# Ordering PSUM evacuations, step pacing and put-off products in a fused attention and MLP kernel

## The chip, the core and the metric

The kernel runs on one core of one Trainium2 chip. The core has five engines that each work through a queue of their own in order: PE (TensorE, matrix products; PEld is its weight load, which overlaps the products), DVE (VectorE), ACT (ScalarE), POOL (GpSimd) and SP (SyncE, which here only issues DMAs). They are ordered among each other by semaphores alone. PE writes its products into PSUM, which has eight banks; here three of them serve as accumulators for the products this document is about. The metric is the device time of one execution in microseconds (us), the median over runs. Times of single instructions come from a profile of one execution.

## The reference

```python
xn = _layernorm(x)                                   # x: 2048 x 640
# A: sliding-window attention, H = 32 heads of Dh = 20, window W = 256
qkv = (xn @ wqkv).reshape(B, S, 3, H, Dh)
scores = jnp.einsum("bhqd,bhkd->bhqk", q, k) * (Dh ** -0.5)
mask = (i - j >= 0) & (i - j < W)
p = _softmax(jnp.where(mask, scores, -1e9))
s = jnp.einsum("bhqk,bhkd->bhqd", p, v) @ wo
# B: MLP with a squared ReLU, F = 1536
h = xn @ w1 + b1
h = where(h > 0, h, 0) ** 2
g = _silu(h @ w2 + b2)
out = x + s * g
```

All tensors are fp32. The kernel splits operands into a high and a low part (hi, lo) and forms three products (hi hi, hi lo, lo hi) for each one of the reference.

## The kernel before

**Stages.** The first 120 us normalise x, transpose it, and compute v for all heads and q, k for the first group of heads. Then a loop of 268 steps (`steps`, L1128) runs the attention of 16 pairs of heads (p), 16 blocks of queries (q) each. In its gaps it runs a filler (L873): the q and k of the other four groups of heads, and then the MLP in eight blocks, each with a first product (hps) and a second one (yps). What comes after the loop is the rest of the filler and the output projection (`out_filler`, wops).

**Row halves.** Within the loop every product has 64 contraction rows. Each is issued as two matmuls, one on rows 0 to 63 of the array (the front) and one on rows 64 to 127 (the back), which can run side by side. The fronts of a job run first. Its backs follow in a queue (`backlog`, for values `urgent`), beside the fronts of the jobs after it.

**The planner's clock.** The order on all engines is written while the program is built. `clock[0]` adds up the estimated cost of the fronts, `clock[1]` that of the backs, from the table COST (L44). `ahead` emits backs until `clock[1]` is LEAD ahead of `clock[0]`, and then one front. None of this exists on the chip: it only decides in which order instructions enter the queues.

**One step (L1149 to L1201).** First the scores of one block (sps), the transposed scores of the block nine steps back (stps), every fourth step the rows of maxima. Then DVE takes the maxima (junk, L503), ACT the exponentials (p, L549), and POOL masks p (L550, L552). Then comes an early piece of filler, then `low` (pl on DVE, L563), `flush()`, `tick()` (splitting of weights), `high` (ph on ACT, L557), then a late piece of filler, and in odd steps the products with v (`values`, ops). p has three buffers; pl is the last to read one. sps and stps have two banks each, both of which every step uses.

**Accumulator banks.** A filler job takes one of three banks (`Acc`, L659), 30 pairs of matmuls for hps (15 for q/k, 18 for yps), and then an evacuation reads the bank:

- q/k: shm on ACT (L112), slo on DVE (L113), two stores.
- hps, in two halves of 256 columns (`part`, L949): relu and hh on ACT, sq on DVE (L956), hl on POOL (L957). The second half is `rest`, in the list `late`.
- yps: one add on DVE (ysb, L990); a store after both halves of a row block.

When the last back of a job is emitted, `done` (L690) puts the evacuation into `pending` and notes the time in `ended`. `soon` (L635), called after each filler product, emits the late half when `clock[0]` is 2 x SOON past the last flush, and a pending evacuation when it is SOON (0.3) past its job's end. `flush` (also called once in the middle of every step) emits all that is waiting. `free` puts a bank back into the list when its evacuation has been emitted.

**Filler per step.** `fill(amount)` draws products until their nominal costs (0.213, 0.1065 and 0.133 a pair) reach the amount: 35% of `per` in the early piece, and 65% plus or minus SWING in the late one. A product whose operand is not evacuated yet (`product`, L1001) yields None, which ends the piece.

Of the kernel before, what the change touches and what calls it, by code (L numbers as in the profile page):

```python
# [16 lines left out]
P = 128  # L17
# [8 lines left out]
NB = 4  # L26
# [12 lines left out]
RAW = 3  # L39
EARLY_FILL = 0.35  # L40
SWING = 0.3
WARM = 22
# [7 lines left out]
LEAD = 0.15  # L50
SOON = 0.3

# [6 lines left out]
def attn_mlp_kernel(ctx: ExitStack, tc, x, wqkv, wo, w1, b1, w2, b2, out):  # L59
# [571 lines left out]

    ended = deque()
    halved = [0.0]

    def soon():  # L635
        now = clock[0]
        if late and now >= halved[0] + 2 * SOON:
            flush(flushed[0])
        if ended and now >= ended[0][1] + SOON:
            flush(ended.popleft()[0])  # L640

    def flush(upto=None):
        halved[0] = clock[0]
        for f in late[:]:
            f()
        late.clear()
        while pending and (upto is None or flushed[0] < upto):
            flushed[0] += 1
            pending.pop(0)()
# [6 lines left out]

    banks = [0, 1, 2]

    class Acc:  # L659

        def __init__(self, n, name):
            while not banks:
                if pending or late:
                    flush()
                else:
                    drain(backlog, 1)
            self.bank, self.n = banks.pop(0), n
            self.tile = pmm.tile([P, n], F32, tag=f"mm{self.bank}", name=name)

        def free(self):  # L670
            banks.append(self.bank)

# [16 lines left out]
    def open_job(evac, *then):  # L689
        def done():  # L690
            pending.append(evac)
            ended.append((mark(), clock[1]))
            for f in then:
                f()
        job = Job(done)
        backlog.append(job)
        return job
# [175 lines left out]
    def filler():  # L873
# [5 lines left out]
        for g, b in order_qk:  # L879
# [9 lines left out]
            for w in "qk":  # L889
                hi, lo = (t() for t in ws[g][w])  # L890
                ps = Acc(BT, "qkps")

                def evac(ps=ps, w=w, g=g, b=b):
# [3 lines left out]
                    split(hi, lo, ps.tile)  # L897
                    ps.free()
                    posts.extend(qk_stores(w, slice(g * P, (g + 1) * P), slice(b * BT, (b + 1) * BT), hi, lo))
# [19 lines left out]
        for n, (hf, b) in enumerate(blocks):  # L919
# [10 lines left out]
            wt1 = w1t[hf]()  # L930
            hs, whole, nxt = {}, set(), []

# [7 lines left out]
            for th in range(2):  # L940
                for fp in range(NFH // 2):
                    ps = Acc(BT, "hps")

                    def evac(ps=ps, th=th, fp=fp, fi=hf * NFH + 2 * fp, hs=hs, whole=whole):
                        hh = [stg.tile([P, BT], F32R, tag="stg", name="hh"),
# [14 lines left out]
                        def rest():  # L960
                            part(1)
                            whole.add((th, fp))
                            ps.free()
                        late.append(rest)
                    job = open_job(evac, *([used] if (th, fp) == (1, NFH // 2 - 1) else []))
                    mms = [(i, lin1(wt1, (wp * KC + c) * FHALF + (2 * fp + i) * P, P), xb[xp][:, c * BT + th * MT:c * BT + (th + 1) * MT]) for i in range(2) for c in range(KC) for wp, xp in ((0, 0), (0, 1), (1, 0))]
# [9 lines left out]
            for tt in range(4):  # L976
# [4 lines left out]
                def start(nh, hf=hf, t=t, place=place, idx=4 * (n - NB) + tt, end=n == NB - 1 and tt == 3, n=n, tt=tt):  # L981
# [3 lines left out]
                    def evac():  # L985
# [4 lines left out]
                        nc.vector.tensor_add(ysb[:, sl], ps.tile, (yins[t] if hf else b2t)[:, sl])  # L990
                        ps.free()
                        if nh:
# [20 lines left out]
                for nh in range(2):  # L1013
                    job = start(nh)
                    for fc in range(NFH):
# [43 lines left out]
    def out_filler(wo_part):  # L1059
# [27 lines left out]
        for u in range(2 * NB):  # L1087
# [10 lines left out]
            for t2 in range(2):  # L1098
# [3 lines left out]
                for nh in range(2):  # L1102
# [21 lines left out]
                    pending.append(evac)  # L1124

    fl = filler()
    total = 8 * (KC - 1) * 15 * 0.213 + 2 * NB * (6 * 15 * 0.213 + 8 * 18 * 0.133)
    steps = NP * NT + LAG + 3  # L1128

    def fill(amount):  # L1130
        state[1] += amount
        while state[0] < state[1]:
            c = next(fl, None)
            if c is None:
                state[1] = state[0]
                return
            state[0] += c
            if state[2] < 10 ** 6:
                soon()

    per = total / (steps - 1)
    with tc.manual_schedule(engines={E_.PE, E_.Activation, E_.DVE, E_.Pool, E_.SP}):
# [6 lines left out]
        for s in range(steps):  # L1149
# [88 lines left out]
```

## Time and profile before

| | us |
|---|---|
| median of 3 runs | 956.03 (954.85 to 958.91) |
| the profiled execution, its own time | 955.41 |
| its span in the profile | 953.7 |
| mean granted clock of PE | 0.991 of full speed |

| stage (us of the span) | what runs |
|---|---|
| 0 to 121 | normalise, transpose, v, first q and k |
| 121 to 288 | attention steps, with the other q and k as filler |
| 288 to 862 | attention steps, with the MLP as filler |
| 862 to 954 | output projection |

How to read the lines that follow: an engine's busy time is given with its share of the span and its count of instructions. A group reads "line engine operation out<-in (partitions x elements)", then its count, its busy time, the mean length of one in ns, the idle time of the engine just before it, and what ended that idle time. A row of a timeline begins with the start and the length in us; "[2.33 <-DVE sq L956]" says that the engine sat idle for 2.33 us until the DVE instruction of line 956 that wrote sq had ended. Rows of one form that follow each other closely are merged (x4). A row of waits gives the total in us, how often, and the longest. The names of the tiles are those of the program: p, ph, pl are the exponentials and their two halves, hps and yps the MLP's accumulators, sps and stps the scores, ops the products with v.

### The profile page before, as it was taken

What the parts mean: (1) busy time and instruction counts of PE and PEld (TensorE: products, weight loads), DVE (VectorE), ACT (ScalarE), POOL (GpSimd) and SP (SyncE); (2) the same over time, 40 slices, a digit from 0 to 9 for tenths busy, and PEclk for the clock granted to TensorE, in tenths of its full rate; (3) what the DMA queues carried; (4) which work ended last, traced back from release to release, by engine and by line L of the source; (5) the groups of instructions that cost most, each with busy time, mean ns of one, the idle gap of its engine ahead of it and who ended that gap; (6) DMA issues with size and microseconds to landing.
All of it is one profiled execution on the core that took longest, in us unless ns stands there. A gap on an engine that the chain in (4) does not pass through costs nothing.

```text
span 953.7 us, 35554 instructions
## 1 busy us (share of the span) xinstructions
PE 898.4 (94%) x14368; PEld 850.3 (89%) x14368; DVE 757.3 (79%) x2085; ACT 648.0 (68%) x1240; POOL 507.4 (53%) x800
## 2 busy tenths in 40 slices
PE   8999999999999989999999889889989989989998
PEld 8999989998888889889899879789889989888998
DVE  7774378998999988878888889978888878864564
ACT  4444347887778967867968867967877967873231
POOL 5010004665556866766867756856776856761000
PEclk9999999999999999999999999999999999999999
DMA  7997788787686262354355244465265274054773
GB/s 250 285 399 276 233 258 255 223 253 252 202 262 193 70 208 85 75 195 112 80 187 147 73 139 121 112 190 151 73 195 156 52 221 124 10 191 142 268 284 126
DMA packets 106108, 169.95 MB, mean 178 GB/s; under 512 B 42072, under 2 KB 59608, under 8 KB 103384
## 3 DMA queue, kind: packets, MB, share of 16 engines
q1 hardware_dynamic: 105944, 167.68, 56.1%
q8 instruction: 113, 1.85, 0.9%
q14 instruction: 51, 0.42, 0.2%
HBM read 96.15 MB, written 70.91 MB: 175 GB/s over the span
## 4 chain that ended last, share of the span: by engine, by line
PE 59%; DVE 20%; ACT 12%; issue 6%; POOL 3%; DMA 0%; DVEq 0%; ACTq 0%; POOLq 0%
PE yps L481 14%; PE ops L481 8%; PE wops L654 7%; PE vps L232 7%; PE qkps L481 6%; DVE junk L503 6%; DVE pl L563 5%; ACT p L549 5%; PE hps L481 5%; PE sps L493 4%; DVE sq L956 3%; PE qkps L209 3%; PE stps L542 3%; ACT relu L953 2%; ACT ph L557 2%
## 5 line engine op out<-in xcount | busy, mean ns | idle before, releaser
L549 ACT ACTIVATE p<-stps,ebias 128x384 f32<-128x384 f32 (+2 forms) x512 | 258.5, 557 | 140.7 <-PE stps L542 62.2
L481 PE MATMUL yps<-w,hh 64*128 64x320 f32 x1536 | 256.9, 320 | 35.1 <-DVE sq L956 24.1
L503 DVE CUSTOM_DVE_ANT_0 junk<-sps,mask 128x384 bf16<-128x384 f32 (+2 forms) x512 | 250.3, 525 | 46.9 <-PE sps L493 30.0
L550 POOL TENSOR_SCALAR_AFFINE_SELECT p<-p 128x256 f32<-128x256 f32 x256 | 151.0, 590 | 234.4 <-ACT p L549 160.6
L563 DVE TENSOR_TENSOR pl<-p,ph 128x768 f16<-128x768 f32 (+2 forms) x256 | 247.8, 968 | 3.5 <-ACT p L549 2.3
L481 PE MATMUL hps<-xb,w 64*128 64x256 f32 x2520 | 236.5, 285 | 2.5 <-DVE ysb L990 2.5
L481 PEld LDWEIGHTS yps<-w,hh 64*128 64x128 f32 x1536 | 197.8, 190 | 43.9 <-DVE sq L956 27.8
L481 PEld LDWEIGHTS hps<-xb,w 64*128 64x128 f32 x2520 | 221.1, 187 | 4.1 <-DVE ysb L990 4.1
L557 ACT ACTIVATE ph<-p 128x768 f16<-128x768 f32 (+2 forms) x256 | 205.7, 804 | 0.0
L481 PE MATMUL ops<-vp,ph 64*128 64x61 bf16 x2880 | 203.8, 190 | 0.1
L481 PE MATMUL ops<-vp,pl 64*128 64x61 bf16 x2880 | 201.7, 189 | 0.0
L481 PE MATMUL yps<-w,hl 64*128 64x320 f32 x768 | 193.4, 320 | 0.0
L481 PEld LDWEIGHTS <-pl 64*128 64x128 f16 x2880 | 177.1, 94 | 0.1
L481 PEld LDWEIGHTS <-ph 64*128 64x128 f16 x2880 | 174.4, 94 | 2.2 <-PE stps L542 0.6
L552 POOL TENSOR_SCALAR_AFFINE_SELECT p<-p 128x256 f32<-128x256 f32 x224 | 133.6, 596 | 0.0
L493 PE MATMUL sps<-ks,qs 60*128 60x384 f32 (+2 forms) x512 | 124.7, 366 | 8.4 <-DVE mrow L526 3.7
L481 PEld LDWEIGHTS yps<-w,hl 64*128 64x128 f32 x768 | 122.9, 189 | 0.0
L542 PE MATMUL stps<-qs,ks 62*128 62x384 f32 (+2 forms) x512 | 110.7, 344 | 0.3 <-DMA qs<-mrow 0.2
L481 PE MATMUL qkps<-xT,wgkh 64*128 64x512 f32 x320 | 103.8, 400 | 0.0
L957 POOL TENSOR_TENSOR hl<-sq,hh 128x256 fp32r<-128x256 f32 x96 | 88.2, 925 | 29.0 <-DVE sq L956 23.5
L481 PE MATMUL qkps<-xT,wgqh 64*128 64x512 f32 x320 | 103.2, 399 | 0.0
L493 PEld LDWEIGHTS sps<-ks,qs 60*128 60x128 f32 x512 | 69.0, 187 | 24.3 <-DVE mt L503 15.3
(110 smaller groups left out, 1627.0 us busy)
## 6 DMA issues: line engine op xcount, KB each, us to landing
ks<-k_d SPq DMA_DIRECT2D x64, 240.0 KB
qs<-q_d SPq DMA_DIRECT2D x64, 240.0 KB
xb<-xs SPq DMA_DIRECT2D x12, 1280.0 KB
xs<-xT SPq DMA_DIRECT2D x8, 1280.0 KB
y<-ysb SPq DMA_DIRECT2D x32, 320.0 KB
k_d<-shm SPq DMA_DIRECT2D x19, 512.0 KB
q_d<-shm SPq DMA_DIRECT2D x19, 512.0 KB
v_d<-vt SPq DMA_DIRECT2D x8, 976.0 KB
```

The costliest lines, as they stand in the source:

```text
L232: nc.tensor.matmul(ps, xT[xp][b][:, c * BT + t * P: c * BT + (t + 1) * P], wv[wp][:, c, nh * HALF:(nh + 1) * HALF], start=first and m == 0 ...
L481: return nc.tensor.matmul(out, a[r], b_[r], skip_group_check=True, **kw)
L493: nc.tensor.matmul(r[hh][:, :nk], qs[i][o, q * P:(q + 1) * P], ks[i][o, k0 * P:k0 * P + nk], start=True, stop=True)
L503: nc.vector.tensor_tensor_reduce(out=junk[:, :nk], in0=r[hh][:, :nk], in1=mask[:, 3 * P - nk:], scale=1.0, scalar=-3.0e38, op0=ALU.add, op ...
L542: nc.tensor.matmul(r[hh][:, :n], ks[i][o, kb * P:(kb + 1) * P], qs[i][o, kb * P:kb * P + n], start=True, stop=True)
L549: nc.scalar.activation(p32[:, hh, :n], r[hh][:, :n], AF.Exp, scale=SCALE, bias=ebias)
L550: nc.gpsimd.affine_select(p32[:, :, 0:P], p32[:, :, 0:P], pattern=[[0, 2], [1, P]], compare_op=ALU.is_ge, fill=0.0, base=0, channel_multip ...
L552: nc.gpsimd.affine_select(p32[:, :, 2 * P:], p32[:, :, 2 * P:], pattern=[[0, 2], [-1, P]], compare_op=ALU.is_gt, fill=0.0, base=0, channel ...
L557: nc.scalar.activation(ph[:, :, :n], p32[:, :, :n], AF.Copy)
L563: nc.vector.tensor_sub(pl[:, :, :n], p32[:, :, :n], ph[:, :, :n])
L654: nc.tensor.matmul(ps, a, b_, start=j == 0, stop=j == n - 1)
L957: nc.gpsimd.tensor_sub(hh[1][:, sl], sq, f32(hh[0][:, sl]))
```

## The change

- `done` no longer queues the evacuation while the steps run: it flushes what is waiting, issues the stores that are posted, and emits the evacuation at once, right behind the job's last back. `ended` is gone.
- The late half of an hps evacuation is emitted when `clock[0]` is SOON (now 0.4) past the first half; before, 2 x 0.3 past the last flush.
- `free(after)` notes the time on the planner's clock at which the bank is likely free (2.0 after the evacuation's emission for q/k, 1.6 for the others); `Acc` takes the bank that comes free first, and moves `clock[0]` to that time.
- `room()`, called ahead of every `Acc` in the filler, yields None while no bank is due within PATIENCE (0.5) of `clock[0]`.
- `fill(upto)` draws products until `clock[0]` reaches a point: 0.4 of the step's pace for the early piece, the end of the step for the late one, less the 24 products of `values` in odd steps. A None moves `clock[0]` there. `pace` is the estimated cost of all filler and attention over the steps. SWING is gone.
- A product whose operand is not evacuated yet yields None without a flush during the steps.
- `ready` asks for one more step; the flag `whole` keeps both clocks going in the output projection.

```diff
@@ constants
-EARLY_FILL = 0.35
-SWING = 0.3
+EARLY_FILL = 0.4
@@
-SOON = 0.3
+SOON = 0.4
+PATIENCE = 0.5
@@ soon, flush
-    ended = deque()
     halved = [0.0]
 
     def soon():
-        now = clock[0]
-        if late and now >= halved[0] + 2 * SOON:
+        if late and clock[0] >= halved[0] + SOON:
             flush(flushed[0])
-        if ended and now >= ended[0][1] + SOON:
-            flush(ended.popleft()[0])
 
     def flush(upto=None):
-        halved[0] = clock[0]
         for f in late[:]:
@@ banks
-    banks = [0, 1, 2]
+    banks = [(0.0, j) for j in range(3)]
+
+    def room():
+        while state[2] < 10 ** 6 and not (banks and banks[0][0] < clock[0] + PATIENCE):
+            yield None
 
     class Acc:
...
-            self.bank, self.n = banks.pop(0), n
+            (at_, self.bank), self.n = banks.pop(0), n
+            clock[0] = max(clock[0], at_)
...
-        def free(self):
-            banks.append(self.bank)
+        def free(self, after):
+            banks.append((clock[0] + after, self.bank))
+            banks.sort()
@@ open_job
         def done():
-            pending.append(evac)
-            ended.append((mark(), clock[1]))
+            if state[2] < 10 ** 6:
+                flush()
+                post_all()
+                evac()
+            else:
+                pending.append(evac)
@@ filler: the same line ahead of all three Acc
+                yield from room()
                 ps = Acc(BT, "qkps")
...
-                    ps.free()
+                    ps.free(2.0)
@@ filler, hps
                         def rest():
                             part(1)
-                            whole.add((th, fp))
-                            ps.free()
+                            made.add((th, fp))
+                            ps.free(1.6)
                         late.append(rest)
+                        halved[0] = clock[0]
@@ filler, yps
-                        ps.free()
+                        ps.free(1.6)
...
-                    while (tt // 2, fc // 2) not in whole:
-                        if pending or late:
+                    while (tt // 2, fc // 2) not in made:
+                        if state[2] < 10 ** 6:
+                            yield None
+                        elif pending or late:
                             flush()
-                            yield None
@@ end of the filler
         ensure("o")
+        whole[0] = True
         yield from out_filler(wo_part)
...
-        return state[2] >= NP * NT - NT + 4 * (u // 2) + 3 + LAG + 5
+        return state[2] >= NP * NT - NT + 4 * (u // 2) + 3 + LAG + 6
@@ fill
-    total = 8 * (KC - 1) * 15 * 0.213 + 2 * NB * (6 * 15 * 0.213 + 8 * 18 * 0.133)
     steps = NP * NT + LAG + 3
-
-    def fill(amount):
-        state[1] += amount
-        while state[0] < state[1]:
+    pace = (8 * (KC - 1) * 15 * COST[BT] + 4 * NB * (3 * 30 * COST[MT] + 4 * 18 * COST[HALF]) + NP * (2 * NT * COST[3 * P] + 12 * NT * COST[61])) / (steps - 1)
+
+    def fill(upto):
+        while clock[0] < upto:
             c = next(fl, None)
             if c is None:
-                state[1] = state[0]
+                clock[0] = upto
                 return
-            state[0] += c
+            if whole[0]:
+                clock[:2] = [clock[0] + c] * 2
             if state[2] < 10 ** 6:
                 soon()
-    per = total / (steps - 1)
@@ the step
-            fill(EARLY_FILL * per)
+            fill((s + EARLY_FILL) * pace)
...
-            fill((1 - EARLY_FILL) * per + SWING * (-1) ** (s - LAG - 3))
             if e and e[1] % 2:
+                fill((s + 1) * pace - 24 * COST[61])
                 values(*e)
+            else:
+                fill((s + 1) * pace)
```

More of the change, by code (lines that the diff above doesn't have):

```diff
@@ L930, in filler @@
             wt1 = w1t[hf]()
-            hs, whole, nxt = {}, set(), []
+            hs, made, nxt = {}, set(), []
             def used(n=n, b=b, nxt=nxt):
@@ L941, in filler, with evac @@
                 for fp in range(NFH // 2):
+                    yield from room()
                     ps = Acc(BT, "hps")
-                    def evac(ps=ps, th=th, fp=fp, fi=hf * NFH + 2 * fp, hs=hs, whole=whole):
+                    def evac(ps=ps, th=th, fp=fp, fi=hf * NFH + 2 * fp, hs=hs, made=made):
                         hh = [stg.tile([P, BT], F32R, tag="stg", name="hh"),
@@ L1013, in filler @@
                 for nh in range(2):
+                    yield from room()
                     job = start(nh)
@@ L1124, in out_filler @@
                     pending.append(evac)
+    whole = [False]
     fl = filler()
-    total = 8 * (KC - 1) * 15 * 0.213 + 2 * NB * (6 * 15 * 0.213 + 8 * 18 * 0.133)
     steps = NP * NT + LAG + 3
-    def fill(amount):
-        state[1] += amount
-        while state[0] < state[1]:
+    pace = (8 * (KC - 1) * 15 * COST[BT] + 4 * NB * (3 * 30 * COST[MT] + 4 * 18 * COST[HALF]) + NP * (2 * NT * COST[3 * P] + 12 * NT * COST[61])) / (steps - 1)
+    def fill(upto):
+        while clock[0] < upto:
             c = next(fl, None)
             if c is None:
-                state[1] = state[0]
+                clock[0] = upto
                 return
-            state[0] += c
+            if whole[0]:
+                clock[:2] = [clock[0] + c] * 2
             if state[2] < 10 ** 6:
                 soon()
-    per = total / (steps - 1)
     with tc.manual_schedule(engines={E_.PE, E_.Activation, E_.DVE, E_.Pool, E_.SP}):
```

## The prediction

> **What bounds the kernel now.** I read the page first (shares, then the chain that ended last), then busy time by stage, then who waited for whom on the matrix engine, then the timeline around the longest of those waits.
>
> ```profile
> span 953.7 us, 35554 instructions
> PE 898.4 (94%) x14368; PEld 850.3 (89%) x14368; DVE 757.3 (79%) x2085; ACT 648.0 (68%) x1240; POOL 507.4 (53%) x800
> PE 59%; DVE 20%; ACT 12%; issue 6%; POOL 3%; DMA 0%; DVEq 0%; ACTq 0%; POOLq 0%
> ```
>
> PE is the bound, and no DMA is on the chain. The next rows cut the span into the steps that carry the later q/k products, the steps that carry the MLP, and the tail with the output projection; the columns are length, busy time of PE, PEld, DVE, ACT and POOL, granted clock, DMA share, GB/s.
>
> ```profile
> 121.00:288.00 167.00, 164.30 (x2410) 149.60 (x2410) 148.78 (x436) 126.05 (x227) 87.29 (x147) 1.00 0.78 245
> 288.00:862.00 574.00, 529.62 (x10551) 503.05 (x10550) 489.04 (x1387) 448.96 (x864) 399.29 (x618) 0.99 0.45 131
> 862.00:953.70 91.70, 86.43 (x653) 85.26 (x649) 45.89 (x92) 22.03 (x34) 1.50 (x3) 1.00 0.61 209
> ```
>
> PE idles 2.7 us in the first, 44.4 us in the MLP stage and 5.3 us in the tail. So the MLP stage is where this change can earn. What PE waits for there:
>
> ```profile
> PE yps L481 <- DVE sq L956: 24.1, 15, 2.6
> PE yps L481 <- DVE ysb L990: 10.6, 15, 2.2
> PE hps L481 <- DVE ysb L990: 2.5, 5, 0.9
> ```
>
> (us, times, longest.) sq is the last reader of an hps bank and ysb the last reader of a yps bank: a product waits for its accumulator bank, not for its operands. These 37.2 us are 84% of the stage's idle PE time.
>
> **The change, part by part.**
>
> *Second half of an hps evacuation.* The wait that ended at 406.53, from the last product in the bank to the first product that reuses it:
>
> ```profile
> 402.12 0.28 PE L481 MATMUL hps<-xb,w 64*128 64x256 f32 x1
> 402.63 0.84 ACT L557 ACTIVATE ph<-p 128x768 f16<-128x768 f32 x1
> 403.38 0.46 ACT L953 ACTIVATE relu<-hps,b1t 128x256 f32<-128x256 f32 x1
> 404.19 1.03 ACT L549 ACTIVATE p<-stps,ebias 128x384 f32<-128x384 f32 x2
> 405.12 0.47 ACT L953 ACTIVATE relu<-hps,b1t 128x256 f32<-128x256 f32 x1
> 406.00 0.47 DVE L956 SCALAR_TENSOR_TENSOR sq<-hps,b1t,relu 128x256 f32<-128x256 f32 x1
> 406.53 0.57 PE L481 MATMUL yps<-w,hh 64*128 64x320 f32 x4 [2.33 <-DVE sq L956]
> ```
>
> The product ends at 402.40, the bank is free at 406.47: 4.1 us. The first relu is behind a ph (0.84) that is ordered ahead of it under either rule, so it does not move. The second relu stands behind the next step's pair of exponentials, from 404.19 to 405.12 = 0.93 us start to start. Now it is ordered 0.3 + 2x0.3 = 0.9 of the planner's clock after the last product; after the change 0 + 0.4. That half us of clock is enough to keep it in the same fill, ahead of that pair. I went through the 15 waits (first and last below, the last with the same pair in between): in ten the pair stands between the two halves, in two ahead of the first half, in three nothing moves, and every wait of the twelve is longer than 0.93.
>
> ```profile
> 329.64 0.41 PE L481 MATMUL yps<-w,hh 64*128 64x320 f32 x1 [0.51 <-DVE sq L956]
> 835.06 1.03 ACT L549 ACTIVATE p<-stps,ebias 128x384 f32<-128x384 f32 x2
> 837.09 0.59 PE L481 MATMUL yps<-w,hh 64*128 64x320 f32 x1 [2.60 <-DVE sq L956]
> ```
>
> Term 1: 12 x 0.93 = **-11.2 us**; ends 0 and -24.1.
>
> *The yps evacuation.* It is one DVE add. Now it is ordered 0.3 of clock after the last product, or at the next flush:
>
> ```profile
> 349.55 0.52 PE L481 MATMUL yps<-w,hh 64*128 64x320 f32 x4
> 351.20 0.56 DVE L503 CUSTOM_DVE_ANT_0 junk<-sps,mask 128x384 bf16<-128x384 f32 x1 [0.22 <-PE sps L520]
> 352.43 0.47 DVE L990 TENSOR_TENSOR ysb<-yps,b2t 128x320 f32<-128x320 f32 x1
> 352.95 0.42 PE L481 MATMUL yps<-w,hh 64*128 64x320 f32 x2 [0.69 <-DVE ysb L990]
> ```
>
> The four merged products at 349.55 contain the bank's last. The add comes 1.23 us late because the next step's maxima (351.20 to 352.43, with their casts) are in front. When a last product is emitted among the scores or the values of a step, no soon() is called before the next maxima; after the change the add goes in at once. Of the 20 waits for ysb (first and last here), 15 have such a pair, or a pl, in front. Each gives up the smaller of itself and about 1.2 us, together 8.1; the other five, 0.80 and the longest (2.2) among them, stay.
>
> ```profile
> 339.72 0.42 PE L481 MATMUL yps<-w,hh 64*128 64x320 f32 x2 [0.45 <-DVE ysb L990]
> 859.08 0.42 PE L481 MATMUL yps<-w,hh 64*128 64x320 f32 x1 [0.80 <-DVE ysb L990]
> ```
>
> Term 2: **-8.1 us**; ends 0 and -13.1 (10.6 + 2.5).
>
> *The granted clock.* The long waits cost more than their length:
>
> ```profile
> 538.59 0.41 PE L481 MATMUL yps<-w,hh 64*128 64x320 f32 x1 [1.81 <-DVE sq L956]
> 566.40 0.41 PE L481 MATMUL yps<-w,hh 64*128 64x320 f32 x1 [2.08 <-DVE ysb L990]
> 625.56 0.63 PE L481 MATMUL yps<-w,hh 64*128 64x320 f32 x1 [2.36 <-DVE sq L956]
> 407.10:410.50 3.40, 3.40 (x52) 3.11 (x51) 0.24 (x1) 0.07 (x1) 0.84 (x1) 0.50 0.98 359
> 540.30:543.60 3.30, 3.30 (x44) 3.30 (x41) 2.47 (x8) 3.08 (x6) 1.69 (x2) 0.50 0.01 2
> 567.60:570.90 3.30, 3.30 (x52) 3.00 (x49) 2.04 (x7) 1.78 (x4) 1.00 (x1) 0.50 0.97 286
> 625.60:628.90 3.30, 3.30 (x24) 3.30 (x26) 0.48 (x1) 0.61 (x2) 0.81 (x2) 0.50 0.88 344
> 837.20:840.50 3.30, 3.30 (x43) 3.30 (x44) 2.09 (x3) 1.06 (x2) 3.19 (x5) 0.50 0.00 0
> ```
>
> Five stretches of 3.3 to 3.4 us at clock 0.50, each right after a wait of 1.81 to 2.60 us. Half speed for 3.4 us loses up to 1.7 us; five lose 8.5. All five waits are among those that terms 1 and 2 shorten, by 0.93 or 1.2; the longest is 1.7 then, below every one that came before such a stretch. Term 3: ends 0 and -8.5; I take three of the five, **-5 us**, since a wait of 2.2 elsewhere left the clock alone, so that chance in their placing has a part. The Trainium skill (TensorE: Matmul & The Clock Gate, Part 1) says that the clock falls to half after about 3.4 us without activity, in a free-running window. The length of the stretches agrees (3.4), the cause does not: no wait here reaches 3.4, and 1.81 came before one. By the page these waits could not be the cause, term 3 would be nought and the sum 940.
>
> *What the earlier evacuations push back.* They go ahead of maxima, pl or exponentials on in-order queues, and PE waits for those too:
>
> ```profile
> PEld sps L493 <- DVE mt L503: 7.0, 22, 1.4
> PEld sps L493 <- DVE mt L503: 7.7, 25, 0.6
> ACT p L549 <- DVE pl L563: 24.0, 26, 1.4
> L113 DVE TENSOR_TENSOR slo<-qkps,shm 128x512 fp32r<-128x512 f32 x38 | 26.1, 688 | 22.6 <-ACT shm L112 22.4
> ```
>
> (First and third row: 121 to 288; second: 288 to 862.) In the MLP stage 25 of some 200 steps have PE held by maxima, one in eight: 30 adds moved ahead of them, at 0.48, are 30 x 0.48 / 8 = 1.8. In the q/k stage it is 22 of 62 steps, a third, and no bank is waited for, so a moved slo (0.69) can only lose: a third of 32 evacuations, 11 x 0.69 / 3 = 2.5. Term 4: **+4 us**; ends 0 and +38, the upper one being 30 x 0.48 for maxima and 48 pieces (one in four of 192) x 0.5 ahead of a pl, whose end the next exponentials need for their buffer, all in full on PE's path.
>
> An evacuation ordered right behind its last product also waits for it if ACT or DVE get there first, with ph, pl or the next exponentials and maxima queued behind, and behind these the selects on POOL and PE's next stps. In the example ACT reaches its first relu 1 us after the product, so no new wait arises there; what of it arises elsewhere lies within the upper end of term 4, since it delays the same pl and exponentials. What is late next, once the banks are home, is the sps bank (maxima), in one step of eight as counted.
>
> *Edits at nothing.* The new pace is (452.5 of filler + 175.6 of attention) / 267 steps = 2.35 of clock a step. The old total of filler is 408.8 in its own costs, 1.53 a step with 0.3 of swing, and a factor of 452.5 / 408.8 = 1.1 turns these into COST: 0.34 + 1.83 x 1.1 = 2.36 in even and 0.34 + 0.68 + 1.23 x 1.1 = 2.38 in odd steps. It is the same load, except that steps at a head pair's edge and the first nine get some 0.3 more filler. That only moves work on a busy PE; if the cover of PE's own work were missing, it would be the tail's idle 5.3 us at most, either way. room() puts products off when no bank is due within 0.5: following the kernel's clock through the order that it builds now, the new rule's free time lies 0.5 behind a request once in 141 reuses, so this part hardly acts, and the clock jumps add up to 2. post_all() in done() issues stores of earlier evacuations half a step sooner on SP's queue; the chain has 0% DMA. ready() one step later delays two loads by about 2.4 us, under the last yps products.
>
> Sum against the profiled execution, 955.41 (span 953.7): 955.4 - 11.2 - 8.1 - 5 + 4 = **935**. The median of the runs shown is 956.03, 0.6 above; within their spread, so I leave 935.
>
> **The rivals.** A change of 0.5%, 4.8 us, is about what a measurement here can tell from none.
>
> *All bank waits go.* Moved halves bring each bank home 1 us sooner, the backlog of second row-halves shortens too, and later waits shrink with the earlier ones: 955.4 - 37.2 - 8.5 + 4 = 914. For it: the waits come in trains, one late bank after another. Against it: relu starts 1 us or more after the product in the example with nothing new moved.
>
> *The gain turns into other waits.* DVE is busy 489 of 574 us and ACT 449; PE's pauses let them catch up. If half of the 24.3 us comes back as waits for maxima or exponentials: 955.4 - 12 + 4 = 947.
>
> *The clock stretches stay*, tied to PE's mean activity and not to these waits: 955.4 - 19.3 + 4 = 940. Against it: all five sit within 2 us behind such a wait. The rule of the Trainium skill's page named above would have it so.
>
> *It does not do what it says.* The evacuation is emitted earlier, yet stands behind the same ph or exponentials as the first relu above, so waits stay: 955.
>
> *Slower.* DVE's order decides: maxima to sps bank, pl to exponentials. A piece ahead of pl delays pl, that the exponentials, that the next stps. In full: terms 1 and 2 are earned, 38 is paid, 955.4 - 19.3 + 38 = 974; it turns slower as soon as over half of the 38 is paid, since 19.3 is earned, and a clear loss at 24; midway between 24 and 38 it is 967. For it: 24.0 us of ACT waiting for pl already. Against it: in the MLP stage ACT waits far longer for PE.
>
> **How the numbers follow.** Forecast 935: 0.43, own range 926 to 945. All waits go: 0.16. Other waits: 0.17. Clock stays: 0.05. Nothing: 0.06. Slower: 0.13. Faster by over 0.5% = 0.43 + 0.16 + 0.15 + 0.05 = 0.79 (0.02 of the third falls within), same 0.08, slower 0.13. The range runs from 911, which takes in most of the first rival, to 956, which takes in the third and fifth; left out are the slower case and the rest of the first, 0.18 in all.
>
> **What would show it.** Right: PE's waits for sq near 13 us and for ysb near 5; a second relu directly behind the first hh in most blocks, ysb ahead of a pair of maxima; at most two stretches at clock 0.50; MLP stage some 550 long with PE idle about 24. Wrong: waits for sq and ysb unchanged (the evacuations were not late by order); PE's or PEld's waits for mt, or stps waiting for p, grown by over 10 us (term 4 was too small); filler left over after the last exponentials, which would mean that put-offs act after all.

## The result, and the profile after

The changed kernel takes 929.0 us (median of 4 runs, 926.8 to 933.6), the kernel before 955.4 beside it: a ratio of 0.9723 [0.9679, 0.9767]. The forecast was 935. The profiled execution took 926.82 us. The page of the changed kernel (span, busy time, chain by engine):

```profile
span 924.8 us, 35572 instructions
...
PE 891.6 (96%) x14368; PEld 846.9 (92%) x14368; DVE 746.7 (81%) x2085; ACT 649.6 (70%) x1240; POOL 510.2 (55%) x800
...
PE 62%; DVE 17%; ACT 12%; issue 4%; DMA 3%; POOL 1%; SPq 0%; DVEq 0%; ACTq 0%; POOLq 0%
```

The span is 28.9 us shorter. PE's idle time, span less busy, went from 55.3 to 33.2 (-22.1), and its busy time from 898.4 to 891.6 (-6.8) for the same 14,368 products. The MLP stage moved as well; from the first hps to the last yps it looks so before and then changed (length, busy time of PE, PEld, DVE, ACT and POOL, granted clock, DMA share, GB/s):

```profile
288.50:867.00 578.50, 534.07 (x10585) 507.24 (x10581) 489.35 (x1389) 448.96 (x864) 399.29 (x618) 0.99 0.45 131
```

```profile
278.40:830.70 552.30, 529.31 (x10629) 505.67 (x10625) 486.69 (x1412) 455.49 (x873) 408.92 (x631) 1.00 0.46 135
```

The stage is 26.2 us shorter, and PE idles 23.0 us in it, where it idled 44.4. Who waited for whom in the changed kernel (us in total, times, longest), and the waits for maxima and pl in the kernel before:

```profile
PE yps L481 <- DVE sq L963: 9.4, 10, 2.1
PE sps L493 <- DVE mrow L526: 6.4, 11, 1.4
PE sps L493 <- DVE mt L503: 4.6, 10, 0.9
...
PE yps L481 <- DVE ysb L998: 1.5, 3, 0.6
...
PEld sps L493 <- DVE mt L503: 18.3, 53, 1.1
...
ACT p L549 <- DVE pl L563: 53.1, 73, 1.8
```

```profile
PE sps L493 <- DVE mrow L526: 3.7, 8, 0.7
PE sps L493 <- DVE mt L503: 3.2, 9, 1.1
...
PEld sps L493 <- DVE mt L503: 15.3, 48, 1.4
...
ACT p L549 <- DVE pl L563: 42.0, 53, 1.4
```

The waits for banks (sq and ysb) fell from 37.2 to 10.9, by 26.3, against 19.3 in the forecast. PE's waits for maxima rose from 3.2 to 4.6 (mt) and for their rows from 3.7 to 6.4 (mrow), PEld's from 15.3 to 18.3, and the exponentials wait for pl 53.1 instead of 42.0: these were pushed back.

Of the order that the prediction wanted to see, one part is there. A yps evacuation now stands directly ahead of a step's maxima in 47 of 64 cases, before in 23 (start, length, engine, line, operation):

```profile
346.75 0.47 DVE L998 TENSOR_TENSOR ysb<-yps,b2t 128x320 f32<-128x320 f32 x1
347.16 0.56 DVE L503 CUSTOM_DVE_ANT_0 junk<-sps,mask 128x384 bf16<-128x384 f32 x1
```

The other part is there in half. The second relu of an hps evacuation stands directly behind the first hh in 26 of 48 cases, before in 15; but the next step's pair of exponentials, which term 1 wanted out of the way, stands between the two halves in 22, before in 18.

Following each bank from its last product to the end of its evacuation, an hps bank comes free after 3.46 us in the median (4.12 before), a yps bank after 1.21 (2.02). And two stretches at half clock are left of five; the first follows the one long wait that stayed, the second comes as the output projection begins. Timeline and windows of the changed kernel:

```profile
729.95 0.41 PE L481 MATMUL yps<-w,hh 64*128 64x320 f32 x1 [2.08 <-DVE sq L963]
```

```profile
730.60:734.00 3.40, 3.40 (x63) 3.12 (x59) 3.33 (x12) 2.31 (x5) 1.30 (x4) 0.51 0.68 171
836.50:839.90 3.40, 3.40 (x21) 3.31 (x18) 1.78 (x3) 2.49 (x4) 1.49 (x3) 0.50 1.05 423
```

Most of this suits the prediction. One thing speaks for another cause: the program's own clock, followed through the build, shows that `room()` put a product off twice (steps 153 and 178, each ahead of the third yps job of an MLP block, which takes the bank of the block's last hps job) and that `Acc` moved the clock four times, by 1.2 in all. Two events in 268 steps look like nothing. The experiments ask whether they are.

### The profile page after: what moved, and what is told of

It reads as the page before. It is cut to its first block, busy times and chain, and to the rows that moved or that the text cites. A ratio compares the mean times of both kernels' runs of the same rounds, so it can differ in the third digit from the quotient of the medians.

```text
span 924.8 us, 35572 instructions
## 1 busy us (share of the span) xinstructions
PE 891.6 (96%) x14368; PEld 846.9 (92%) x14368; DVE 746.7 (81%) x2085; ACT 649.6 (70%) x1240; POOL 510.2 (55%) x800
## 3 DMA queue, kind: packets, MB, share of 16 engines
q8 instruction: 113, 1.85, 0.8%
## 4 chain that ended last, share of the span: by engine, by line
PE 62%; DVE 17%; ACT 12%; issue 4%; DMA 3%; POOL 1%; SPq 0%; DVEq 0%; ACTq 0%; POOLq 0%
PE yps L481 13%; PE ops L481 8%; PE wops L649 8%; PE vps L232 8%; PE hps L481 8%; DVE junk L503 5%; PE qkps L481 5%; ACT p L549 5%; DVE pl L563 4%; PE sps L493 4%; PE qkps L209 3%; PE stps L542 3%; DVE sq L963 3%; ACT relu L960 2%; ACT ph L557 2%
## 5 line engine op out<-in xcount | busy, mean ns | idle before, releaser
L549 ACT ACTIVATE p<-stps,ebias 128x384 f32<-128x384 f32 (+2 forms) x512 | 259.0, 559 | 109.7 <-DVE pl L563 53.1
L503 DVE CUSTOM_DVE_ANT_0 junk<-sps,mask 128x384 bf16<-128x384 f32 (+2 forms) x512 | 249.6, 523 | 17.3 <-PE sps L493 15.3
L481 PE MATMUL yps<-w,hh 64*128 64x320 f32 x1536 | 249.5, 314 | 11.0 <-DVE sq L963 9.4
L563 DVE TENSOR_TENSOR pl<-p,ph 128x768 f16<-128x768 f32 (+2 forms) x256 | 242.7, 948 | 5.9 <-PE ops L481 5.6
L481 PE MATMUL hps<-xb,w 64*128 64x256 f32 x2520 | 234.0, 284 | 0.1
L481 PEld LDWEIGHTS yps<-w,hh 64*128 64x128 f32 x1536 | 193.5, 185 | 14.8 <-DVE sq L963 12.2
L481 PE MATMUL yps<-w,hl 64*128 64x320 f32 x768 | 183.3, 312 | 0.0
L493 PE MATMUL sps<-ks,qs 60*128 60x384 f32 (+2 forms) x512 | 128.2, 368 | 12.7 <-DVE mrow L526 6.4
L481 PEld LDWEIGHTS yps<-w,hl 64*128 64x128 f32 x768 | 117.5, 185 | 0.0
L964 POOL TENSOR_TENSOR hl<-sq,hh 128x256 fp32r<-128x256 f32 x96 | 85.4, 891 | 31.1 <-DVE sq L963 29.5
L481 PE MATMUL qkps<-xT,wgkh 64*128 64x512 f32 x320 | 101.3, 395 | 0.0
L493 PEld LDWEIGHTS sps<-ks,qs 60*128 60x128 f32 x512 | 71.6, 185 | 31.2 <-DVE mt L503 18.3
```

What stands on the lines that cost most here:

```text
L481: return nc.tensor.matmul(out, a[r], b_[r], skip_group_check=True, **kw)
L493: nc.tensor.matmul(r[hh][:, :nk], qs[i][o, q * P:(q + 1) * P], ks[i][o, k0 * P:k0 * P + nk], start=True, stop=True)
L503: nc.vector.tensor_tensor_reduce(out=junk[:, :nk], in0=r[hh][:, :nk], in1=mask[:, 3 * P - nk:], scale=1.0, scalar=-3.0e38, op0=ALU.add, op ...
L549: nc.scalar.activation(p32[:, hh, :n], r[hh][:, :n], AF.Exp, scale=SCALE, bias=ebias)
L563: nc.vector.tensor_sub(pl[:, :, :n], p32[:, :, :n], ph[:, :, :n])
L964: nc.gpsimd.tensor_sub(hh[1][:, sl], sq, f32(hh[0][:, sl]))
```

## The experiments

Two theories. **Order**: the earlier evacuations are the whole gain, the rest is nothing. **Pace and put-offs**: products held back while no bank is free earn a part of it, or all. A table of all kernels comes first. The kernels ran in four comparisons, each with the kernel before beside it (955.4 to 957.6), and the ratio is to that one. The other columns come from one profiled execution of each kernel. Idle is span less PE's busy time; bank waits are PE's idle time ahead of the products of yps and hps, nearly all of it waits for sq and ysb (in e6, e8, e12 and e13 1.1 to 1.5 us of it are not); score waits are its idle time ahead of sps and stps; "half clock" is the time at a granted clock of 0.5 within the profile, its last 2 us left out; put-offs are counted as the order is built.

| kernel | median us | ratio to before [95%] | PE busy | idle | bank waits | score waits | half clock | put-offs |
|---|---|---|---|---|---|---|---|---|
| before | 955.4 | 1 | 898.4 | 55.3 | 37.6 | 9.1 | 17.0 | - |
| changed | 929.0 | 0.9723 [0.9679, 0.9767] | 891.6 | 33.2 | 11.0 | 13.4 | 6.8 | 2 |
| e4_yps_only | 942.4 | 0.9844 [0.9800, 0.9888] | 891.4 | 47.4 | 29.5 | 9.6 | 17.0 | - |
| e5_hps_only | 951.1 | 0.9928 [0.9904, 0.9952] | 901.9 | 47.3 | 29.0 | 11.3 | 17.0 | - |
| e1_order_only | 937.6 | 0.9791 [0.9752, 0.9830] | 892.5 | 42.6 | 19.8 | 14.7 | 10.2 | - |
| e3_no_room | 937.8 | 0.9795 [0.9754, 0.9836] | 894.6 | 36.1 | 14.1 | 12.0 | 13.6 | 0 |
| e6_pace_no_room | 949.0 | 0.9930 [0.9908, 0.9952] | 895.3 | 50.5 | 33.1 | 7.3 | 17.0 | 0 |
| e2_pace_only | 922.5 | 0.9633 [0.9596, 0.9670] | 890.2 | 29.1 | 11.9 | 9.1 | 0 | 9 |
| e9_room_no_jump | 922.4 | 0.9650 [0.9621, 0.9679] | 888.8 | 30.9 | 15.4 | 8.8 | 6.8 | 8 |
| e11_putoff_alone | 920.6 | 0.9623 [0.9600, 0.9646] | 891.2 | 27.9 | 12.2 | 7.8 | 0 | 7 |
| e12_more_putoffs | 921.9 | 0.9642 [0.9616, 0.9667] | 898.1 | 24.2 | 6.3 | 8.5 | 10.2 | 20 |
| e7_later_banks | 926.8 | 0.9685 [0.9646, 0.9724] | 895.0 | 31.4 | 5.7 | 16.7 | 13.6 | 5 |
| e8_qk_old_order | 930.0 | 0.9726 [0.9696, 0.9756] | 892.6 | 36.1 | 11.6 | 14.7 | 13.6 | 2 |
| e13_pace_yps_now | 917.4 | 0.9593 [0.9566, 0.9620] | 886.4 | 27.3 | 12.5 | 7.9 | 0 | 5 |

### Order without pace, pace without order

e1 is the kernel before with the new order of evacuations and nothing else:

```diff
-SOON = 0.3
+SOON = 0.4
...
-        if late and now >= halved[0] + 2 * SOON:
+        if late and clock[0] >= halved[0] + SOON:
...
-            pending.append(evac)
-            ended.append((mark(), clock[1]))
+            if state[2] < 10 ** 6:
+                flush()
+                post_all()
+                evac()
```

> The kernel before, with only the order of evacuations changed: at once at a job's last back, late half 0.4 of clock after the first half. Fill, pace and bank list stay as before. Theory 'order': about 930 to 936 us, waits for sq near 10 and for ysb near 2. Rival 'pacing' (the clock that ends each step brings the gain): above 948.

e2 is the changed kernel with the old order back (`pending`, `ended`, 2 x SOON past the last flush, SOON 0.3), so with the new fill, the times of the banks and `room()`:

```diff
...
-                flush()
-                post_all()
-                evac()
+            pending.append(evac)
+            ended.append((mark(), clock[1]))
```

> The changed kernel with the old order of evacuations (pending and ended, SOON 0.3, late half 2 x SOON past the last flush); pace, fill, room() and the bank list with its times stay as changed. Theory 'order': 948 to 958 us, waits for sq and ysb together still over 28. Rival 'pacing': 930 to 938.

Measured: e1 937.6 and e2 922.5. e1 comes out near where the prediction's sum stood (935), just above its own 930 to 936. e2, without any of the order, falls below both of its ranges and beats the changed kernel. Waits of e1, then of e2:

```profile
PE yps L481 <- DVE sq L955: 14.6, 11, 2.0
PE sps L493 <- DVE mt L503: 6.5, 11, 1.4
PE yps L481 <- DVE ysb L990: 5.1, 5, 1.8
...
PEld sps L493 <- DVE mt L503: 23.2, 65, 1.6
```

```profile
PE yps L481 <- DVE sq L964: 9.8, 13, 1.6
PE sps L493 <- DVE mrow L526: 4.2, 10, 0.9
PE sps L493 <- DVE mt L503: 3.0, 8, 1.2
...
PE yps L481 <- DVE ysb L998: 1.6, 3, 0.7
```

e1's 14.6 and 5.1 come close to the prediction's "near 13" and "near 5", at the price of waits for maxima (mt 3.2 to 6.5, PEld 15.3 to 23.2). e2 has shorter waits for banks still, and no more for maxima than before. So "order is all" falls; order is one way to the gain, and pace and put-offs are another that earns more.

### Each evacuation by itself

e4 emits only the yps evacuation at once, e5 only that of hps (with its second half 0.4 after its first); both start from the kernel before.

```diff
+            if now and state[2] < 10 ** 6:
+                flush(flushed[0])
+                evac()
...
-                    return [ps, open_job(evac), 0]
+                    return [ps, open_job(evac, now=True), 0]
```

> The kernel before, with only the yps evacuation emitted at once. Theory 'order', by term 2 of the prediction: 955 less 8 to 11 gives 944 to 948, waits for ysb under 3, waits for sq near 24. Rival 'trains' (one late bank makes the next late): the waits for sq fall too, below 20, and the time is under 944.

```diff
-        if late and now >= halved[0] + 2 * SOON:
+        if late and now >= halved[0] + 0.4:
...
+                        halved[0] = clock[0]
-                    job = open_job(evac, *([used] if (th, fp) == (1, NFH // 2 - 1) else []))
+                    job = open_job(evac, *([used] if (th, fp) == (1, NFH // 2 - 1) else []), now=True)
```

> The kernel before, with only the hps evacuation emitted at once and its second half 0.4 of clock later. By term 1: 955 less 11 to 15, and up to 5 for the clock, gives 936 to 944, waits for sq 9 to 13, waits for ysb near 13. Rival 'trains': the waits for ysb fall too, below 9.

Measured: 942.4 and 951.1. Waits of e4, then of e5:

```profile
PE yps L481 <- DVE sq L960: 24.1, 15, 2.6
...
PE yps L481 <- DVE ysb L994: 5.2, 5, 2.2
```

```profile
PE yps L481 <- DVE sq L959: 14.9, 11, 2.1
PE yps L481 <- DVE ysb L994: 11.2, 16, 2.1
PE sps L493 <- DVE mt L503: 5.3, 11, 1.3
PE hps L481 <- DVE ysb L994: 2.5, 5, 0.9
```

In e4 ysb fell from 13.1 to 5.2 and sq stayed to the tenth: 7.9 off the waits, as in term 2 (8.1). The time is under the 944 to 948 that term 2 gave, but the rival 'trains' fails too, since the waits for sq did not fall. The profiled time fell by 14.8 (955.41 to 940.60), of it 7.9 in idle and 7.0 in busy time, with as much half clock as before. In e5 the waits for sq fell by 9.2, but score waits took 2.2 of it back and busy time rose by 3.5, so that the profiled time fell by 4.5. By the medians the gain is 6.5 us, and 951.1 misses the 936 to 944 expected. All of the order together gains 20.0 in e1 (957.6 to 937.6, the medians of that comparison). That the hps part is worth as much as its waits is refuted; why busy time goes up in one and down in the other isn't settled.

### The put-offs taken away

e3 is the changed kernel without `room()`'s two put-offs and without the clock's move in `Acc`; e6 is e2 with the same edit.

```diff
-PATIENCE = 0.5
+PATIENCE = 1e9
...
-            clock[0] = max(clock[0], at_)
```

> The changed kernel without put-offs and without the move of the clock to a bank's time (PATIENCE without bound, the max in Acc gone). In the changed kernel room() acts twice in all and the clock is moved by 1.2 in four places, so: within 3 us of the changed kernel, 926 to 932. If it is over 935, the bank's clock does more than its count says.

> The kernel of e2_pace_only (new pacing, old order of evacuations) without put-offs and without the move of the clock. Theory 'put-offs': in e2 room() acted nine times, once at nearly every change from hps to yps, and that took the bank waits away; without it 932 to 945 us and waits for sq over 18. Rival 'absolute clock': the fill up to a point on the clock alone does it; 920 to 926, waits for sq near 10.

Measured: 937.8 and 949.0. e3 missed its 926 to 932: without two put-offs and four moves of the clock the changed kernel falls back to the time of order alone (e1, 937.6). Their worth is 8.8 us by the medians; the intervals of the two ratios overlap, so the size is loose. The profiled executions lie 5.8 apart, with 3.1 us less of waits for banks in the changed kernel and 6.8 less at half clock. The waits for banks in e3:

```profile
PE yps L481 <- DVE sq L962: 8.4, 8, 1.8
...
PE yps L481 <- DVE ysb L997: 5.4, 5, 2.7
```

Between e6 and e2 the difference is 26.5, with intervals far apart; e6 misses its 932 to 945 by 4, on the side away from its rival. The waits of e6 beside those of e2 above:

```profile
PE yps L481 <- DVE sq L963: 21.5, 16, 3.1
PE yps L481 <- DVE ysb L997: 7.5, 13, 1.7
...
PE hps L481 <- DVE ysb L997: 1.8, 3, 0.8
```

That is 30.8 us of waits for banks, where e2 has 11.6. These four kernels make a square, all with the new pace: neither 949.0, order 937.8, put-offs 922.5, both 929.0. Order earns 11.2 without put-offs and loses 6.5 with them (the intervals of these two ratios lie only just apart). The counts suggest one reason: a bank evacuated earlier looks free earlier on the planner's clock, so `room()` acts twice with the new order and nine times with the old one, at least once in each of the eight MLP blocks, a few steps behind the change from hps to yps.

e9 tells the put-offs from the clock's move in `Acc` (e2 without the move):

```diff
-            clock[0] = max(clock[0], at_)
```

> The kernel of e2_pace_only (922.5 us) with put-offs but without the move of the clock to a bank's time in Acc; room() then acts eight times. Theory 'put-offs': within 4 us of e2, 919 to 927. Rival 'clock in Acc': over 935, as in e6_pace_no_room (949).

Measured: 922.4, the same as e2 with 922.5. So in e2 it is the put-offs.

### The put-offs alone

e11 is the kernel before, with its old fill and its old order, plus the times of the banks, the clock's move in `Acc` and `room()`; a put-off moves the planner's clock by the filler that is given up.

```diff
-    banks = [0, 1, 2]
+    banks = [(0.0, j) for j in range(3)]
+    def room():
+        while state[2] < 10 ** 6 and not (banks and banks[0][0] < clock[0] + 0.5):
+            yield None
...
+            (at_, self.bank), self.n = banks.pop(0), n
+            clock[0] = max(clock[0], at_)
...
+                    yield from room()
                     ps = Acc(BT, "hps")
...
+                clock[0] += 1.1 * (state[1] - state[0])
                 state[1] = state[0]
```

> The kernel before, with its old order of evacuations and its old fill by amounts, and only the bank list with times and room() added (a put-off moves the clock by 1.1 of the amount given up). room() acts seven times, at four of the eight changes from hps to yps. Theory 'put-offs do it by themselves': about half of what e2 gains over e6 (26), so 936 to 946. Rival 'put-offs need the pace on the absolute clock': over 950.

Measured: 920.6, far better than expected: seven put-offs, with eight moves of the clock by 2.2 in all, earn 36 us (956.5 before in that comparison) with neither the new pace nor the new order. That the moves add nothing is known for e2 alone (e9). The timelines of PE at the first change from hps to yps show how. Before:

```profile
333.72 0.30 PE L481 MATMUL yps<-w,hl 64*128 64x320 f32 x1
...
336.02 0.56 PE L481 MATMUL yps<-w,hh 64*128 64x320 f32 x3 [1.85 <-DVE sq L956]
...
337.31 0.47 PE L493 MATMUL sps<-ks,qs 60*128 60x384 f32 x2
337.48 0.47 PE L542 MATMUL stps<-qs,ks 62*128 62x384 f32 x2
```

And e11:

```profile
333.77 0.31 PE L481 MATMUL yps<-w,hl 64*128 64x320 f32 x1
333.92 0.39 PE L493 MATMUL sps<-ks,qs 60*128 60x384 f32 x1
333.96 0.54 PE L542 MATMUL stps<-qs,ks 62*128 62x384 f32 x2
334.67 0.56 PE L481 MATMUL yps<-w,hh 64*128 64x320 f32 x4 [0.16 <-DVE sq L964]
```

Before, the yps front stands at the head of PE's queue for 1.85 us, and the next step's scores, which need no accumulator bank, are stuck behind it, and with them the maxima and exponentials that need these scores. In e11 the front is put off to the next step, the scores go first, and what is left of the wait is 0.16. What happens to the banks shows when each is followed through the order and the trace: for yps, the time from the last front of a job to the first of its remaining backs is 2.67 us in the mean before, 2.38 in e6, 1.16 in e11 and 1.13 in e2; a step that takes no new front works its backs off. A yps bank is held for 13.2 us before, 11.2 in e11 and in e2, 11.0 in the changed kernel. There the saving is split: the evacuation takes 1.31 instead of 1.92, the lag 1.60. So order and put-offs shorten the hold of a yps bank at different ends, which may be why they do not add. For hps it is otherwise: a bank is held for 16.3 us before, 16.2 in e11 and 16.5 in e2. The 13.9 us of waits for sq that e11 spares do not come from banks that are free sooner; its products ask for them later.

### How much of each

e12 puts off more (e2 with PATIENCE 0 and hps banks 0.5 later), e7 gives the changed kernel later times for its banks, e8 returns q/k alone to the old order in the changed kernel, and e13 is e2 with only the yps evacuation at once.

```diff
-PATIENCE = 0.5
+PATIENCE = 0.0
...
-                            ps.free(1.6)
+                            ps.free(2.1)
```

> The kernel of e2_pace_only with PATIENCE 0 and hps banks 0.5 later: twenty put-offs in place of nine, 10.0 of clock given up in place of 5.1. Theory 'put-offs turn into loss once the bank waits are gone': 922 to 930 us, waits for sq under 5, more filler behind the last exponentials. Rival 'more is better': under 920.

```diff
-                            ps.free(1.6)
+                            ps.free(2.1)
...
-                        ps.free(1.6)
+                        ps.free(1.9)
```

> The changed kernel with later times for its banks: free(2.1) for hps and free(1.9) for yps in place of 1.6, the times that the old order implied. room() then acts five times and the clock moves in eight places. Theory 'put-offs': 922 to 926 us, waits for sq below 8. Rival 'order in the q/k stage' (the changed kernel loses to e2 in the q/k stage only): 928 to 930, no change.

```diff
+        if ended and clock[0] >= ended[0][1] + 0.3:
+            flush(ended.popleft()[0])
...
-        job = open_job(evac, *then)
+        job = open_job(evac, *then, now=False)
```

> The changed kernel with the old order for the q/k evacuations alone (pending, 0.3 of clock after the job's end); hps and yps as changed. By term 4 in the q/k stage, which took 162.0 us from the first scores to the first hps in the changed kernel and 158.6 in e2: 924 to 927 us, and that stage 158 to 160. If it stays at 929, the q/k order costs nothing at the end.

```diff
-                        ps.free(1.6)
+                        ps.free(1.9)
...
-                    return [ps, open_job(evac), 0]
+                    return [ps, open_job(evac, now=True), 0]
```

> The kernel of e2_pace_only with the yps evacuation alone emitted at once, its bank time 1.9 to make up for that; room() acts five times. If the order of the yps evacuation still earns with put-offs in place: 915 to 921 us. If put-offs and order earn the same waits, only once: 921 to 927.

Measured: e12 921.9, no gain over e2. Its waits for sq and ysb fell from 11.6 to 4.4, but more filler came after the last exponentials, where the tail grew from 94.8 to 102.2 us, and it has 10.2 us at half clock where e2 has none: more put-offs brought nothing more. e7 926.8, between its two ranges and not to be told from the changed kernel; waits for sq fell to 3.4 and those for mt doubled to 9.1. e8 930.0, where 924 to 927 was expected; its windows from the first scores to the first hps and on to the last exponentials can be set beside those of the changed kernel, 162.0 and 555.5 us: it took 158.8 and 560.9. What the q/k stage gained came back in the MLP stage, and why is open. e13 917.4, the fastest of all and faster than the kernel before and the changed one. It lies in the range for an order of yps that still earns, but beside e2 the intervals overlap. Its waits:

```profile
PE yps L481 <- DVE sq L968: 9.2, 11, 1.6
...
PE sps L493 <- DVE mt L503: 2.5, 8, 1.1
```

e7 and e13 both have five put-offs. They differ in what is emitted at once: hps, yps and q/k in e7, yps alone in e13; and besides in SOON and in the time of an hps bank. Score waits are 16.7 in the one and 7.9 in the other, and these 8.8 us are nearly the 9.4 between their times. As e8 still has 14.7 with q/k undone, this points to the hps evacuation, whose two halves go ahead of maxima, pl and exponentials. It is not shown: no run undid the hps part alone in the changed kernel.

## Why the prediction was right, and where it was wrong

The sign and the size held: 929.0, forecast 935, range 911 to 956. The kernel moved by 26.4 against 20.4 forecast.

**Terms 1 and 2, the evacuations: right as a sum, wrong in the split.** With order alone (e1) the waits for sq fell by 9.5 and for ysb by 8.0; the forecast had 11.2 and 8.1, and the time was 937.6. Apart, the yps evacuation was worth 15 us (8.1 forecast; its waits were exact, its saving in busy time was not seen), and the hps evacuation 6.5 (11.2 forecast). That the two errors cancel in the sum is luck. Term 1 was too large for two reasons. In e5 as in e1 the pair of exponentials still stands between the halves in 15 of 48 evacuations (18 before), so the half us of clock did not keep the second half ahead of it as often as term 1 had it (12 of 15 waits). And a wait's length was taken for its worth, while part of it went on to the maxima.

**Term 3, the clock: right in size, loosely tied to its cause.** Three of five stretches went, as forecast, in the profiled executions; the four runs of the changed kernel have mean clocks of 0.993 to 0.996, where ten runs of the kernel before had 0.983 to 0.991. But e4 and e5 have as much half clock as before, in other places, though e4 spares most of the waits for ysb and e5 much of those for sq. A stretch isn't owed to the length of one wait; the last section shows what it goes by, and why the wait of 2.2 that the prediction saw left the clock alone.

**Term 4, what is pushed back: right in size as a sum.** +4 forecast; score waits rose by 4.3 in the changed kernel and by 5.6 in e1. But the q/k stage alone cost more than its part. There, where 2.5 was forecast, the windows from the first scores to the first hps, before and in e1:

```profile
118.00:288.50 170.50, 167.63 (x2427) 152.15 (x2428) 151.18 (x444) 127.35 (x230) 87.29 (x147) 1.00 0.77 240
```

```profile
116.20:292.00 175.80, 170.12 (x2427) 154.09 (x2428) 152.85 (x446) 130.22 (x235) 85.28 (x147) 0.99 0.76 240
```

The same 2,427 products take 5.3 us longer, 1.7 of it a stretch at half clock; e4 and e5, without the q/k part, take 170.7 and 170.6. But e8 shows that undoing it in the changed kernel brought nothing at the end.

**Edits at nothing: this is the step that failed.** The new pace was rightly put at nothing beside the new order (e3 and e1: 937.8 and 937.6), though alone it is worth 7 (e6). `room()` was put at nothing because it would act about once in 141 reuses. The count was right, it acted twice; its price was not. The prediction asked how often a put-off happens, not what one is worth. The put-offs fall where a yps job is to take a bank of the last hps jobs, and the timelines of e11 show one sparing PE a wait with the scores behind it. Two of them with the clock's moves were worth 8.8 us here by the medians, nine 26.5 (e6 to e2), and seven with the clock's moves 36 (e11). The sign that the prediction set for put-offs, filler left over after the last exponentials, did not come: 85 products of yps ran behind them before, and none in the changed kernel.

**Rivals.** "All bank waits go" (914) did not come: 26.3 of the 37.2 us went, not all. "Other waits" was there in part: 4.3 us of score waits. "The clock stays" fell with three stretches gone. "Slower" did not come: nothing like 24 of its 38 us was paid. "It does not do what it says" fell with the waits.

Open: why e11 gains with seven put-offs what e2 gains with nine and the new pace; what in busy time follows the waits; and what took e8's gain back. No run gave up as much filler at other steps, so that the place of a put-off matters, and not only the lighter step, is argued from the timelines.

## What to carry to other kernels

Here a product that waited for its bank at the head of PE's queue also held up the scores behind it that need none (1.85 us in the example). In such a place look first whether the product can be put off, and then whether the evacuation can be hurried, for the hurried evacuation pushed back the maxima that feed the next step. Price a rare action by what one of it may be worth, not by its count. Run each part of such a change alone and in pairs: here order and put-offs earned largely the same waits, and the change as a whole (929.0) lost to one of its halves (922.5).

## What was unexpected of the hardware

The waits of e4 cost more than their length, and more than the clock explains: it spared 7.9 us of idle time and 7.0 of busy time at the same time at half clock, with the same products. In e5, which spared others, busy time rose. The ends of the products are modelled, so the profile can't say why.

The length of a single wait does not decide on the half clock. Of the waits that the prediction showed, 1.81 was the shortest ahead of a stretch; in e7 one of 1.35 was followed by one, and in e6 one of 3.09 was not. Timeline and windows of e7, then of e6:

```profile
326.23 1.08 PE L493 MATMUL sps<-ks,qs 60*128 60x384 f32 x2 [1.35 <-DVE mt L503]
```

```profile
326.80:330.20 3.40, 3.40 (x35) 3.40 (x37) 3.24 (x7) 2.30 (x4) 3.32 (x7) 0.50 0.93 379
```

```profile
819.51 0.41 PE L481 MATMUL yps<-w,hh 64*128 64x320 f32 x1 [3.09 <-DVE sq L963]
```

```profile
814.50:817.90 3.40, 1.92 (x24) 1.66 (x21) 2.80 (x12) 3.31 (x7) 2.81 (x6) 1.00 0.03 7
817.90:821.30 3.40, 1.79 (x40) 1.79 (x42) 1.84 (x4) 1.73 (x4) 2.88 (x4) 1.00 0.00 0
819.50:823.00 3.50, 3.49 (x64) 3.46 (x64) 1.98 (x6) 1.98 (x5) 1.96 (x4) 1.00 0.13 23
```

The trace's record of the clock shows what goes with a stretch. In the kernel before each of the five is 3.413 us long, and their starts (407.10, 540.22, 567.52, 625.55, 837.17) are 39, 8, 17 and 62 times 3.413 us apart: they sit on one grid. On this grid the interval just ahead of each holds 1.79 to 2.60 us of idle PE. The wait of 3.09 in e6 falls across a boundary, at 817.9, and leaves 1.5 us on one side and 1.6 on the other; so does the wait of 2.2 in the kernel before, at 552.2, with 0.4 and 1.8. Over the attention steps of all fourteen kernels each of the 15 intervals at full clock with more than 1.85 us of idle PE is followed by a stretch; of those between 0.98 and 1.85 16 are and 95 are not, and what tells these apart is open. From run to run the share of half clock differs: ten runs of the kernel before have mean clocks from 0.983 to 0.991, and the slowest (962.9) has the lowest.

In e2, e11 and e13, whose longest waits for banks are 1.5 or 1.6, the MLP stage has no such stretch at all. All this fits a free-running window that judges how busy PE was in it; the Trainium skill (TensorE: Matmul & The Clock Gate, Part 1) describes such a window of about 3.4 us. The stretches agree with its length, but its demand of a whole window without work does not agree with 1.35.
